# An early one-element Exp, an earlier sum of gelu halves, score banks for a late attention, and a last pair in four banks

## The chip, the cores and the metric

The kernel runs on one core of a Trainium2 chip. The metric is the device time of one execution in microseconds (us). The kernel before was timed three times: 299.24, 299.31 and 299.81 us, median 299.31. Engine names are those of the profile: PE (matmul; PEld is its weight load), DVE (vector), ACT (activation), POOL (GpSimd) and SP, which here only issues DMAs.

## The reference

Attention with a sliding window and 32 global tokens over 8 batches and 8 heads of 64, then a two-layer perceptron with a quick gelu on all 4352 tokens:

```python
s_g   = scale * q_g @ k_all^T            # 32 global rows see all 544 keys
out_g = softmax(s_g) @ v_all
s_l   = [scale * q_l @ k_g^T, where(|i - j| <= 32, scale * q_l @ k_l^T, -1e9)]
out_l = softmax(s_l) @ [v_g, v_l]
x = concat(out_g, out_l) as (B * S, H * D)    # 4352 x 512
h = x @ w_in                                  # 512 -> 2048
g = h / (1 + exp(-1.702 h))
out = g @ w_out                               # 2048 -> 512
```

## The kernel before, in words

The work is cut into phases. A batch i has 512 local tokens. In the first half of its phase (`h_step`, lines 630 to 636) PE makes `hp` for each of 16 slices of d_ff with the weights `w_in_sb` (line 613), and ACT takes each through the gelu into `gT` (line 618). In the second half (`phase_o`, lines 991 to 1046, for i = 2 to 6) PE makes the output of batch i and the attention of batch i+1 and part of i+2, interleaved by hand. The instructions go to each engine in the order in which the Python code writes them (`tc.manual_schedule()`), so a line that stands earlier is earlier in its engine's queue. After batch 7 there is a last stage of the global tokens of all batches (i = B, half as wide), into which the output of batch 7 is interleaved (lines 1082 to 1105), and then one last pair (lines 1107 to 1118).

**The output pairs.** The second matmul layer is done in blocks of two by two with seven products in place of eight. `Pair(i, tt)` has products 1 to 7 (`mm`, line 712), each eight matmuls of 128x256, with sums of gelu halves (`g_sums`, lines 686 and 689, on DVE; index 0, 1, 2 or 3 by line 684) and of weights (`wsum`) as operands. Two PSUM banks hold the four accumulators: `px` has products 3 and 5 in its first half and 4 and 2 in its second, `py` has 1 and 7 in its first half and 6 in its second. Intermediate values are read out between: `m3` (ACT copies product 3 to `zz`, line 113 by way of `on_act`), `z` (line 724, DVE adds the other half of px), `zm` (line 727, adds py), `sub` (line 734), `evict` (ACT copies px to `ob`, line 731, shown as 113), `add` (line 737), `store` (lines 739 to 750: eight DMAs of 32 rows, all issued by SP). Product 5 writes px again, so it waits for `z`; product 7 writes py again and needs g_sums index 3, and waits for `zm`.

**The attention.** `S` (line 558) makes the scores of a group of four heads in the score banks (`spair`), `X` (line 569) takes their Exp on ACT, `M` (line 574) multiplies by the mask, on POOL for round 0 of the later groups (3.3 us) and on DVE for round 1 of the second group (1.0 us). `U(0)` to `U(2)` (line 584) multiply by ones and by the two halves of v, into banks named `ov`, `Gm` (line 595) does the global rows into `og`. `R` (lines 460 to 464) turns the sums of U(0) into reciprocals, `XL` (line 469) scales U(1) and U(2) into `xL`, `G` (lines 474 to 477) does the global rows.

**Banks and tables.** PSUM has eight banks: four in the pool `psP` (`pbank`: hp, px, py, ov, og take turns) and four score banks. A tile that takes a bank waits for the readers of the one before it. ACT loads a table when the function changes between Exp and gelu (1.28 us). `gelu_table` (line 623) calls a gelu on one element to place that load ahead of the next h_step; for Exp the load stands with the first `X` of a phase and takes over its wait.

Of the kernel before, what the change touches and what calls it, by code (L numbers as in the profile page):

```python
# [12 lines left out]
F32 = mybir.dt.float32  # L13
BF16 = mybir.dt.bfloat16
FP8 = mybir.dt.float8e4
AF = mybir.ActivationFunctionType
# [4 lines left out]
def kernel(  # L21
# [12 lines left out]
    nc = tc.nc  # L34

    B, H, Sl, D = q_l.shape
    Sg = q_g.shape[2]
    S = Sg + Sl
    n_tokens = B * S
    d_model = H * D  # L40
# [7 lines left out]
    FC = d_ff // 128  # L48
# [12 lines left out]
    moe = ctx.enter_context(tc.tile_pool(name="moe", bufs=1))  # L61
# [29 lines left out]
    def load_v(b, hs=slice(0, 8)):  # L91
        if b == 2:
            nc.gpsimd.memset(v_view(b, 5)[:, :, :, :, D:], 1.0)
        vt = v_view(b, 5).rearrange("p u j c d -> p (u j) c d")
        vs, vg = (x[b].rearrange("h s d -> s h d") for x in (v_l, v_g))
        for c in range(5):
            n = 128 if c == 2 else 96
            nc.gpsimd.dma_start(out=vt[0:n, hs, c, :D], in_=vs[FIRST[c] : FIRST[c] + n, hs])  # L98
            if c != 2 and b != 1:
                nc.gpsimd.dma_start(out=vt[96:128, :, c, :D], in_=vg)  # L100
# [11 lines left out]
    def on_act(out_, in_):  # L112
        nc.scalar.activation(out_, in_, AF.Copy)  # L113
# [49 lines left out]
    for j in range(4):  # L163
        r = (j + 1) % 4
        nc.gpsimd.memset(bd[32 * r : 32 * r + 32, j, :], 1.0)
    for i in range(2):
# [3 lines left out]
        out=step, in_=step, pattern=[[1, 289]], compare_op=ALU.is_ge,  # L170
# [108 lines left out]
    def pbank(name):  # L279
        return psP.tile([128, 512], F32, name=name, tag="p")  # L280


    def spair():
        return [psS.tile([128, 2, 512], F32, name="s4", tag="s%d" % i) for i in range(2)]

    def bank(pair, j):
        return pair[j // 2][:, j % 2, :]
# [318 lines left out]
    def width(i):  # L606
        return TB if i < B else B * Sg
# [9 lines left out]
    def gelu(out_, in_):  # L617
        nc.scalar.activation(out_, in_, AF.Gelu_apprx_sigmoid)  # L618

    spot = consts.tile([128, 2], F32)  # L620
    nc.gpsimd.memset(spot, 0.0)

    def gelu_table():
        gelu(spot[:, 0:1], spot[:, 1:2])

    def h_act(i, fc, hp):
        n = width(i)
        gelu(gTs[i][:, fc, :n], hp[:, :n])
# [22 lines left out]
    HM = d_model // 2  # L651
# [13 lines left out]
    def parts_of(i):  # L665
        n = width(i)
        t = gTs[i].rearrange("p (g e) t -> p g e t", e=2)
        return [t[:, :, e, h * n // 2 : h * n // 2 + n // 2] for h in range(2) for e in range(2)]

    def g_sums(i, lo, hi, which=(0, 1, 2, 3)):  # L670
        n = width(i)
        if i not in sums:
            if i < B:
                sums[i] = [moe.tile([128, FC // 2, w * HT], BF16, name="gs%d" % k)
                           for k, w in enumerate((1, 1, 2, 1))]
            else:
                room = [ld.tile([128, 2, 16 * D], BF16, name=x).rearrange("p a b -> p (a b)")
                        for x in ("rk", "rq", "rk")]
                sums[i] = [x.rearrange("p (g t) -> p g t", g=FC // 2)
                           for x in (room[0][:, :1024], room[0][:, 1024:], room[1], room[2][:, :1024])]  # L680
        a11, a12, a21, a22 = parts_of(i)
        t = gTs[i].rearrange("p (g e) t -> p g e t", e=2)
        g = slice(lo, hi)
        for k in which:
            if k == 2:
                nc.vector.tensor_tensor(sums[i][2][:, g, :n], t[:, g, 0, :n], t[:, g, 1, :n], ALU.add)  # L686
            else:
                x, y, op = {0: (a11, a22, ALU.add), 1: (a21, a11, ALU.subtract), 3: (a12, a22, ALU.subtract)}[k]
                nc.vector.tensor_tensor(sums[i][k][:, g, : n // 2], x[:, g], y[:, g], op)  # L689

    class Pair:
        def __init__(self, i, tt, banks=None):
            self.i, self.tt = i, tt
            self.banks = banks

        def mm(self, *ks):
            i, tt = self.i, self.tt
            n = width(i) // 2
            a11, a12, a21, a22 = parts_of(i)
            s = sums[i]  # L700
            for k in ks:
                lv, rv, where = {
                    1: (s[0], wsum[0], 2), 2: (s[2][:, :, n : 2 * n], b11, 1), 3: (a11, wsum[1], 0),
                    4: (a22, wsum[2], 1), 5: (s[2], b22, 0), 6: (s[1], wsum[3], 3), 7: (s[3], wsum[4], 2),
                }[k]
                if k == 3:
                    self.x = self.banks[0] if self.banks else pbank("px")
                if k == 1:
                    self.y = self.banks[1] if self.banks else pbank("py")
                out_ = (self.y if where > 1 else self.x)[:, where % 2 * HM : where % 2 * HM + HM]  # L710
                for g in range(FC // 2):
                    nc.tensor.matmul(out_, lhsT=lv[:, g, tt * 128 : tt * 128 + 128], rhs=rv[:, g, :],  # L712
                                     start=(g == 0 and k in (1, 3)), stop=(g == FC // 2 - 1 and k in (2, 5, 6, 7)),
                                     skip_group_check=True)

        def m3(self, eng="act"):
# [19 lines left out]
        def add(self):  # L736
            nc.vector.tensor_add(self.ob[:, 0:4:3], self.zz, self.y.rearrange("p (h m) -> p h m", h=2))

        def store(self):
            for h in range(2):  # L740
                tile_out(self.i, self.tt + h * (width(self.i) // 256), self.ob[:, 2 * h : 2 * h + 2].rearrange("p h m -> p (h m)"))

    def tile_out(i, tci, ob):
        for j in range(4):
            if i < B:
                rows = out[i * S + Sg : (i + 1) * S, :].rearrange("(r t) m -> t r m", t=16)[4 * tci + j]
            else:
                r = (4 * tci + j) * S
                rows = out[r : r + Sg, :]
            nc.sync.dma_start(out=rows, in_=ob[32 * j : 32 * j + 32])  # L750

    obs = {}

# [7 lines left out]
    a, c = Quad(0), Quad(1)  # L761
# [44 lines left out]
    pt = spair()  # L806
# [13 lines left out]
    pt = spair()  # L820
# [27 lines left out]
    a, c = nq[1]  # L848
# [40 lines left out]
    pt = spair()  # L889
# [18 lines left out]
    pt = spair()  # L908
# [3 lines left out]
    a, c = nq[2]  # L912
# [26 lines left out]
    def loads_after(i):  # L939
        if i + 2 < B:  # L940
            load_v(i + 2)
        if i == 1:
            load_g(8, NQ)
        if i + 3 < B:
            load(i + 3)

    def quads_of(n):
        if n < B and n not in nq:
            nq[n] = (Wide(2 * n), Wide(2 * n + 1))
        return nq.get(n, (None, None))  # L950
# [40 lines left out]
    def phase_o(i):  # L991
        b = i + 1
        a, c = nq[b]
        a2, c2 = quads_of(b + 1)
        p0, p1 = Pair(i, 0), Pair(i, 1)
        loads_after(i)
        a.UG()
        c.S(0)
        a.R()
        g_sums(i, 7, 8, (0,))  # L1000
        a.XL(0)
        g_sums(i, 7, 8, (1, 2))
        a.XL(1)
        p0.mm(3, 4, 1)
        c.X(0)
        c.M(0, nc.gpsimd)
        p0.m3()
        p0.z()
        a.G()
        g_sums(i, 7, 8, (3,))  # L1010
        c.S(1)
        c.X(1)
        p0.mm(6)
        p0.zm()
        c.M(1)
        p0.mm(5, 2)
        p0.sub()
        p0.evict()
        p0.mm(7)
        p0.add()  # L1020
        p0.store()
        c.U(0)
        if a2:
            a2.S(0)
            a2.X(0)
            a2.M(0, nc.gpsimd)
        c.U(1)
        c.U(2)
        c.Gm()
        c.RXG()  # L1030
        p1.mm(3, 4)
        p1.m3()
        p1.z()
        p1.mm(1, 6)
        p1.zm()
        if a2:
            a2.S(1)
            a2.X(1)
            a2.M(1, nc.gpsimd)
        p1.mm(5, 2)  # L1040
        p1.sub()
        p1.evict()
        gelu_table()
        p1.mm(7)
        p1.add()
        p1.store()

    for i in range(1, B):
        if i > 1:
            for fc in range(FC):  # L1050
# [3 lines left out]
                if i + 1 < B:  # L1054
                    c = nq[i + 1][1]
# [23 lines left out]
    def pair_banks(k):  # L1079
        return [psX.tile([128, 512], F32, name="x", tag="x%d" % (2 * (k % 2) + j)) for j in range(2)]  # L1080
# [3 lines left out]
    for st in range(FC):  # L1084
        h_step(B, st)
        if st < len(todo):
            tt, k = todo[st]
            if k == 3:
                p = Pair(B - 1, tt, pair_banks(tt))
            p.mm(k)  # L1090
            if k == 4:
                p.m3()
                p.z()
            if k == 6:
                p.zm()
            if k == 2:
                p.sub()
                p.evict()
            if k == 7:
                p.add()  # L1100
                p.store()
        if st in (4, 8, 12):
            g_sums(B, st // 2 - 2, st // 2)
        if st == 14:
            g_sums(B, 6, 7)
    g_sums(B, 7, 8)
    p = Pair(B, 0, pair_banks(0))
    p.mm(3, 4)
    p.m3()
    p.z()  # L1110
    p.mm(1, 6)
    p.zm()
    p.mm(5, 2)
    p.sub()
    p.evict()
    p.mm(7)
    p.add()
    p.store()


# [28 lines left out]
```

## Time and profile before

| what | us |
|---|---|
| median of three runs | 299.31 |
| the profiled execution's own time | 299.64 |
| its span | 297.9 |
| PE busy | 281.3 (94%) |
| DVE busy | 205.1 (69%) |
| ACT busy | 187.9 (63%) |
| POOL busy | 126.7 (43%) |
| ACT table loads | 16, 1.283 each |

The profile is one execution as the hardware profiler saw it. A busy share is that of the whole span. In a timeline each row has the start in us, the duration, the engine, the line, the operation with its tiles and shapes, and in brackets how long the engine had been idle and what ended that. In the chain that ended last, each row is a piece of work, in order of time, that the next one had to wait for. Mean durations of the rows that the change touches: mask on POOL 3.33 (1760 wide), on DVE 1.15 and 1.06; Exp 1.01; product matmul 0.27, starting 0.109 apart; gs of 256 0.25 to 0.28 when nothing holds it; `m3` 0.39, `z` 0.40, `zm` 0.41, `sub` 0.68, `add` 0.69, `evict` 0.60. The phases i = 2 to 6 begin their second half at 102.63, 134.33, about 167.4, about 200.4 and 233.44 us; the last pair's matmuls run from 285.10 to 291.23.

### The profile page before, as it was taken

To read this page: it belongs to the slowest core of one execution; us is meant where nothing else is said; L and a number is where in the kernel's file an instruction comes from. 1 tells how busy PE (TensorE), PEld (TensorE's weight loads), DVE (VectorE), ACT (ScalarE), POOL (GpSimd) and SP (SyncE) were. 2 spreads that over 40 slices of the span, in tenths; PEclk is the share of its full clock that TensorE was granted. 3 is DMA by queue.
4 is the path that set the end of the run, shared out by engine and by line. 5 is a ranking of instruction groups with operands and counts; after the bars stand their busy time and mean duration, and the time that the engine had idled before them with its cause. 6 is when DMAs were issued, how large, how long until landed. Compare 5 with 4: busy or idle time off the path is not lost.

```text
span 297.9 us, 8839 instructions
## 1 busy us (share of the span) xinstructions
PE 281.3 (94%) x3705; PEld 180.3 (61%) x3727; DVE 205.1 (69%) x473; ACT 187.9 (63%) x298; POOL 126.7 (43%) x149
## 2 busy tenths in 40 slices
PE   8899999999999999999999989999999989999990
PEld 7544445444554588547764668447764668458880
DVE  7670268945888997878967986798964886353251
ACT  4857788568677765877468655877377642763320
POOL 8893559786045044952379044923360040000000
PEclk9999999999999999999999999999999999999996
DMA  7999999999959603594129902690121002200222
GB/s 199 163 205 209 204 167 139 188 163 132 197 71 128 116 2 76 87 129 89 29 70 130 150 4 73 97 64 2 47 68 33 2 2 73 70 0 2 70 73 72
DMA packets 59352, 28.24 MB, mean 95 GB/s; under 512 B 47536, under 2 KB 49584, under 8 KB 59312
## 3 DMA queue, kind: packets, MB, share of 16 engines
q0 software_dynamic: 51664, 17.57, 53.5%
q1 hardware_dynamic: 7360, 9.58, 11.7%
q8 instruction: 29, 0.48, 0.7%
q10 hardware_dynamic: 288, 0.52, 0.5%
q14 instruction: 11, 0.09, 0.1%
HBM read 36.31 MB, written 8.91 MB: 152 GB/s over the span
## 4 chain that ended last, share of the span: by engine, by line
PE 69%; DMA 10%; DVE 8%; ACT 4%; POOL 4%; issue 3%; DVEq 0%; POOLq 0%
PE hp L613 33%; PE px L712 7%; PE py L712 7%; PE x L712 6%; PE op L645 6%; PE s L558 4%; PE ov L584 4%; DMA rq<-in_q_l_dram 4%; ACT e L569 3%; DMA w_out_sb<-in_moe_w_out_dram 3%; DVE gs L689 3%; DMA v<-in_v_l_dram 2%; PE s L613 1%; DVE sT L460 1%; DVE xL L469 1%
## 5 line engine op out<-in xcount | busy, mean ns | idle before, releaser
L613 PE MATMUL hp<-xL,w_in_sb 128*128 128x512 bf16 x466 | 104.5, 379 | 1.3 <-DVE xL L469 0.4
L613 PEld LDWEIGHTS <-w_in_sb 128*128 128x128 bf16 x576 | 56.1, 98 | 60.4 <-issue 0.7
L618 ACT ACTIVATE gT<-hp 128x512 bf16<-128x512 f32 x120 | 70.4, 596 | 26.3 <-PE hp L613 24.9
L574 POOL TENSOR_TENSOR e<-e,mask 128x1760 bf16<-128x1760 bf16 (+1 forms) x14 | 46.3, 3304 | 82.7 <-ACT e L569 82.7
L569 ACT ACTIVATE e<-s 128x1016 bf16<-128x1016 f32 (+1 forms) x56 | 53.4, 1006 | 15.2 <-PE s L558 14.8
L689 DVE TENSOR_TENSOR gs<-gT 128x512 bf16<-128x512 bf16 (+1 forms) x90 | 40.2, 472 | 18.8 <-ACT gT L618 18.8
L712 PEld LDWEIGHTS <-gs 128*128 128x128 bf16 x480 | 46.2, 98 | 9.7 <-issue 3.1
L98 POOL DMA_DIRECT2D v<-in_v_l_dram x40 | 31.1, 784 | 16.6 <-PE og L595 12.7
L712 PE MATMUL py<-wsum,gs 128*128 128x256 bf16 x240 | 30.3, 272 | 2.4 <-DVE zz L727 2.4
L645 PE MATMUL op<-w_out_sb,gT 128*128 128x512 bf16 x122 | 28.8, 379 | 0.7 <-issue 0.3
L510 DVE STREAM_TRANSPOSE kT<-rk 128x512 f32<-128x512 f32 x14 | 14.6, 1045 | 9.0 <-DMA rk<-in_k_l_dram 9.0
L645 PEld LDWEIGHTS <-gT 128*128 128x128 bf16 x128 | 11.9, 98 | 14.1 <-issue 0.2
L469 DVE TENSOR_TENSOR xL<-ov,rs 128x512 bf16<-128x512 f32 x29 | 19.1, 685 | 1.0 <-PE ov L436 0.4
L712 PEld LDWEIGHTS <-gT 128*128 128x128 bf16 x192 | 18.0, 98 | 2.8
L712 PE MATMUL px<-w_out_sb,gT 128*128 128x256 bf16 x160 | 19.2, 273 | 0.1
L712 PE MATMUL px<-w_out_sb,gs 128*128 128x256 bf16 x160 | 19.1, 273 | 0.0
L558 PEld LDWEIGHTS <-kT 32*128 32x128 bf16 x672 | 13.3, 93 | 9.6 <-issue 7.4
L113 ACT ACTIVATE ob<-px 128x512 f32<-128x512 f32 x10 | 6.0, 597 | 20.5 <-DVE zz L734 20.5
L574 DVE TENSOR_TENSOR e<-e,mask 128x1712 bf16<-128x1712 bf16 (+1 forms) x14 | 15.7, 1122 | 4.3 <-ACT e L569 4.3
L686 DVE TENSOR_TENSOR gs<-gT 128x1024 bf16<-128x1024 bf16 (+1 forms) x30 | 17.3, 577 | 0.0
L558 PE MATMUL s<-q,kT 32*128 32x160 bf16 (+1 forms) x448 | 15.3, 246 | 0.0
L100 POOL DMA_DIRECT2D v<-in_v_g_dram x24 | 14.1, 589 | 1.6 <-DMA v<-in_v_l_dram 1.6
(140 smaller groups left out, 345.8 us busy)
## 6 DMA issues: line engine op xcount, KB each, us to landing
out_dram<-ob SPq DMA_DIRECT2D x136, 64.0 KB, 1.7
rq<-in_q_l_dram POOLq DMA_DIRECT2D x5, 512.0 KB, 7.3
rk<-in_k_l_dram POOLq DMA_DIRECT2D x5, 512.0 KB, 9.0
v<-in_v_l_dram POOLq DMA_DIRECT2D x24, 96.0 KB, 4.1
w_in_sb<-in_moe_w_in_dram POOLq DMA_DIRECT2D x8, 256.0 KB, 7.9
w_out_sb<-in_moe_w_out_dram POOLq DMA_DIRECT2D x4, 512.0 KB, 10.2
rq<-in_q_l_dram POOLq DMA_DIRECT2D x5, 256.0 KB, 6.2
rk<-in_k_l_dram POOLq DMA_DIRECT2D x5, 256.0 KB, 6.2
```

The costliest lines, as they stand in the source:

```text
L98: nc.gpsimd.dma_start(out=vt[0:n, hs, c, :D], in_=vs[FIRST[c] : FIRST[c] + n, hs])
L469: nc.vector.tensor_mul(self.x[:, 2 * self.u + h, :], self.st[1 + h], self.st["rs"])
L510: nc.vector.transpose(flat[:, 0:Sl].rearrange("p (r t) -> p t r", t=16), loaded[self.b][0][:, self.u].bitcast(F32))
L558: nc.tensor.matmul(bank(self.ps, j)[:, at : at + n], lhsT=self.k[p, KEYS[c] : KEYS[c] + 128, e], rhs=qs[p, :, :, e], start=(e == 0), stop= ...
L569: nc.scalar.activation(self.E[rnd][:, 2 * i : 2 * i + 2, :n], self.ps[i][:, :, :n], AF.Exp, scale=scale)
L574: eng.tensor_mul(e, e, mask[:, rnd : rnd + 1, :n].to_broadcast([128, 4, n]))
L613: nc.tensor.matmul(hp[:, : width(i)], lhsT=w_in_c[:, fc // 4, kc, fc % 4 // 2, :, fc % 2], rhs=(xL[i] if i < B else xG)[:, kc, :], start=( ...
L618: nc.scalar.activation(out_, in_, AF.Gelu_apprx_sigmoid)
L645: nc.tensor.matmul(op, lhsT=gTs[i][:, fc, tci * 128 : tci * 128 + 128], rhs=w_out_sb[:, fc, :], start=(first and fc == 4 * f4), stop=(fc = ...
L686: nc.vector.tensor_tensor(sums[i][2][:, g, :n], t[:, g, 0, :n], t[:, g, 1, :n], ALU.add)
L689: nc.vector.tensor_tensor(sums[i][k][:, g, : n // 2], x[:, g], y[:, g], op)
L712: nc.tensor.matmul(out_, lhsT=lv[:, g, tt * 128 : tt * 128 + 128], rhs=rv[:, g, :], start=(g == 0 and k in (1, 3)), stop=(g == FC // 2 - 1 ...
```

## The change

1. A new `exp_table()` calls an Exp on one element. `phase_o` calls it first, behind the last gelu of the batch.
2. In `phase_o` the sum of index 3 for the last slices (`g_sums(i, 7, 8, (3,))`) moves from behind `a.G()` to directly behind `a.XL(1)`, ahead of `p0.m3()` and `p0.z()`.
3. In the last `phase_o` (i = 6, where there is no further batch), U(0), U(1), U(2) and Gm of the second group go to four score banks instead of `pbank`s.
4. `store` can name the engine that issues each half. The second pair of batch 7 gives its second half to ACT's queue; it is written in step 13 of the last stage, ahead of the gelus of steps 14 and 15.
5. The last pair has four banks, one for each accumulator, the order of products 3, 4, 1, 6, 2, 5, 7 (before: 3, 4, 1, 6, 5, 2, 7), and stores its output in three pieces: the second tile by SP (four DMAs of 64 KB), then the second column half of the first tile by POOL and its first column half by ACT (four of 32 KB each).

```diff
+    def exp_table():
+        nc.scalar.activation(spot[:, 0:1], spot[:, 1:2], AF.Exp)
...
+            self.apart = banks and len(banks) == 4
...
+                if self.apart:
+                    out_ = self.banks[where][:, :HM]
...
-                                     start=(g == 0 and k in (1, 3)), stop=(g == FC // 2 - 1 and k in (2, 5, 6, 7)),
+                                     start=(g == 0 and k in ((1, 3, 4, 6) if self.apart else (1, 3))), stop=(g == FC // 2 - 1 and k in (2, 5, 6, 7)),
...
-        def store(self):
+        def store(self, engs=(nc.sync, nc.sync)):
...
+        def quarter(self, h, m, eng):
+            tile_out(self.i, self.tt + h, self.ob[:, 2 * h + m], eng, slice(m * HM, m * HM + HM))
...
         loads_after(i)
+        exp_table()
         a.UG()
         c.S(0)
         a.R()
...
         a.XL(1)
+        g_sums(i, 7, 8, (3,))
         p0.mm(3, 4, 1)
         c.X(0)
         c.M(0, nc.gpsimd)
         p0.m3()
         p0.z()
         a.G()
-        g_sums(i, 7, 8, (3,))
...
-        c.U(0)
         if a2:
+            c.U(0)
...
+        else:
+            pt = spair()
+            c.U(0, bank(pt, 0))
+            c.U(1, bank(pt, 2))
+            c.U(2, bank(pt, 3))
+            c.Gm(bank(pt, 1))
...
-                p.store()
+                p.store((nc.sync, (nc.sync, nc.scalar)[tt]))
...
-    p = Pair(B, 0, pair_banks(0))
-    p.mm(3, 4)
-    p.m3()
-    p.z()
-    p.mm(1, 6)
-    p.zm()
-    p.mm(5, 2)
-    p.sub()
-    p.evict()
+    x0, y0 = pair_banks(0)
+    y1, x1 = pair_banks(1)
+    p = Pair(B, 0, (x0, x1, y0, y1))
+    zz = [moe.tile([128, HM], F32, name="zz%d" % k) for k in range(2)]
+    p.ob = moe.tile([128, 4, HM], F32, name="ob", bufs=3)
+    p.mm(3)
+    on_act(zz[0], x0[:, :HM])
+    p.mm(4)
+    nc.vector.tensor_add(zz[0], zz[0], x1[:, :HM])
+    p.mm(1)
+    nc.vector.tensor_add(zz[1], zz[0], y0[:, :HM])
+    p.mm(6)
+    nc.vector.tensor_add(zz[1], zz[1], y1[:, :HM])
+    p.mm(2)
+    nc.vector.tensor_sub(p.ob[:, 3], zz[1], x1[:, :HM])
+    on_act(p.ob[:, 2], x1[:, :HM])
+    tile_out(B, 1, p.ob[:, 2:4].rearrange("p h m -> p (h m)"))
+    p.mm(5)
+    nc.vector.tensor_sub(zz[0], zz[0], x0[:, :HM])
+    on_act(p.ob[:, 1], x0[:, :HM])
+    p.quarter(0, 1, nc.gpsimd)
     p.mm(7)
-    p.add()
-    p.store()
+    nc.vector.tensor_add(p.ob[:, 0], zz[0], y0[:, :HM])
+    p.quarter(0, 0, nc.scalar)
```

More of the change, by code (lines that the diff above doesn't have):

```diff
@@ L705, in mm @@
                 }[k]
[L706 to L710, printed above, removed]
+                if self.apart:
+                    out_ = self.banks[where][:, :HM]
+                else:
+                    if k == 3:
+                        self.x = self.banks[0] if self.banks else pbank("px")
+                    if k == 1:
+                        self.y = self.banks[1] if self.banks else pbank("py")
+                    out_ = (self.y if where > 1 else self.x)[:, where % 2 * HM : where % 2 * HM + HM]
                 for g in range(FC // 2):
                     nc.tensor.matmul(out_, lhsT=lv[:, g, tt * 128 : tt * 128 + 128], rhs=rv[:, g, :],
-                                     start=(g == 0 and k in (1, 3)), stop=(g == FC // 2 - 1 and k in (2, 5, 6, 7)),
+                                     start=(g == 0 and k in ((1, 3, 4, 6) if self.apart else (1, 3))), stop=(g == FC // 2 - 1 and k in (2, 5, 6, 7)),
                                      skip_group_check=True)
@@ L737, in add, with tile_out @@
             nc.vector.tensor_add(self.ob[:, 0:4:3], self.zz, self.y.rearrange("p (h m) -> p h m", h=2))
-        def store(self):
+        def store(self, engs=(nc.sync, nc.sync)):
             for h in range(2):
-                tile_out(self.i, self.tt + h * (width(self.i) // 256), self.ob[:, 2 * h : 2 * h + 2].rearrange("p h m -> p (h m)"))
-    def tile_out(i, tci, ob):
+                tile_out(self.i, self.tt + h * (width(self.i) // 256),
+                         self.ob[:, 2 * h : 2 * h + 2].rearrange("p h m -> p (h m)"), engs[h])
+        def quarter(self, h, m, eng):
+            tile_out(self.i, self.tt + h, self.ob[:, 2 * h + m], eng, slice(m * HM, m * HM + HM))
+    def tile_out(i, tci, ob, eng=nc.sync, cols=slice(0, d_model)):
         for j in range(4):
             if i < B:
-                rows = out[i * S + Sg : (i + 1) * S, :].rearrange("(r t) m -> t r m", t=16)[4 * tci + j]
+                rows = out[i * S + Sg : (i + 1) * S, cols].rearrange("(r t) m -> t r m", t=16)[4 * tci + j]
             else:
                 r = (4 * tci + j) * S
-                rows = out[r : r + Sg, :]
-            nc.sync.dma_start(out=rows, in_=ob[32 * j : 32 * j + 32])
+                rows = out[r : r + Sg, cols]
+            eng.dma_start(out=rows, in_=ob[32 * j : 32 * j + 32])
     obs = {}
@@ L1026, in phase_o @@
             a2.M(0, nc.gpsimd)
-        c.U(1)
-        c.U(2)
-        c.Gm()
+            c.U(1)
+            c.U(2)
+            c.Gm()
+        else:
+            pt = spair()
[3 more added lines that the diff above has]
+            c.Gm(bank(pt, 1))
         c.RXG()
```

## The prediction

> **What bounds the kernel now.** I read the page's busy shares first, then the chain that ended last in order of time, then the timelines of DVE, POOL, ACT and SP around the edits.
>
> ```profile
> PE 281.3 (94%) x3705; PEld 180.3 (61%) x3727; DVE 205.1 (69%) x473; ACT 187.9 (63%) x298; POOL 126.7 (43%) x149
> ```
>
> PE is busy 94% of the 297.9 us span, so only what makes PE wait or run longer counts, and what stands behind PE's last matmul. The waits by pair put three kinds of PE wait inside the phases that the diff touches: py behind DVE zz L727 (2.4 us, 4 times), s behind ACT e L569 (1.9 us, 4 times), and 0.32 us behind ACT ob L113, once. The chain shows one of the four phases (i=3):
>
> ```profile
> 135.76 0.63 PE s L558 x23
> 136.53 1.18 issue
> 137.71 1.93 ACT e L569 x2
> 139.63 0.29 ACT zz L113
> 139.94 0.42 DVE zz L724
> ...
> 141.04 2.22 DVE gs L689
> 143.25 0.34 DVE zz L727
> 143.64 1.03 PE py L712 x8
> ```
>
> Two things are to be seen. "issue" is the load of the Exp table, which waits with the first Exp for the scores. And gs L689, 0.25 us elsewhere, takes 2.2. ACT, DVE and POOL say why:
>
> ```profile
> 134.44 0.60 ACT L618 ACTIVATE gT<-hp 128x512 bf16<-128x512 f32 x1 [0.27 <-PE hp L613]
> 136.41 1.28 ACT L569 ACT_TABLE_LOAD   x1 [1.38 <-PE s L558]
> 137.71 1.93 ACT L569 ACTIVATE e<-s 128x1016 bf16<-128x1016 f32 x2
> ...
> 138.19 0.68 DVE L469 TENSOR_TENSOR xL<-ov,rs 128x512 bf16<-128x512 f32 x1
> 140.96 2.29 DVE L689 TENSOR_TENSOR gs<-gT 128x256 bf16<-128x256 bf16 x1
> ...
> 139.79 3.32 POOL L574 TENSOR_TENSOR e<-e,mask 128x1760 bf16<-128x1760 bf16 x1 [8.97 <-ACT e L569]
> ```
>
> POOL masks from 139.79 to 143.11; the DVE sum, with two inputs from SBUF, ends 0.14 us behind it. DVE operations with one input from PSUM (zz L724) run beside POOL at their usual 0.42 us. So a gs that meets a running mask waits until the mask ends.
>
> I count from the start of ov in a phase (134.33 here). Phase i=2 has its table load early by chance (103.35) and lasts 17.79 us (102.63 to 120.42) without a PE wait; phase 3 lasts 19.13. Phases 4 to 6 repeat phase 3's waits. So **1.34 us a phase** is what the table load costs, four times.
>
> **Part 1: the table load.** Last gelu at +0.11, its successor 0.62 later (103.35 behind 102.73), the load 1.28, the one-element Exp 0.11 to its successor (122.38 to 122.49 for the gelu twin). So X(0) starts at +2.13 instead of +3.38; the scores are there at +2.08. In phase 2 it moves from +2.04 to +2.13. POOL's mask starts 2.08 us behind X(0) (139.79 - 137.71): at **+4.21** in every phase.
>
> **Part 2: the sum of halves moved ahead.** g_sums(3) now stands on DVE directly behind xL of half 1 and ahead of zz L724. In phases 2 to 5 DVE works without a gap up to there, and the instruction behind xL starts 0.60 after it (106.49 to 107.09): 138.19 + 0.60 is **+4.46**, 0.25 us behind the new start of the mask. By the rows above it then waits for the mask: the mask ends at 4.21 + 3.32 = 7.53, gs at 7.67, zz L724 starts at 7.60 (0.07 overlap, as L727 today), and PE can go on 0.46 later (143.18 to 143.64), at 8.06. Who waits for zz L724? In the order of the changed program the first px matmul of product 5 does, as before; it was ready at +6.11 in phase 2 (108.74) and +6.79 in phase 3. Products 5 and 2 take 1.86 (108.74 to 110.60), so product 7 starts at 9.92. Today it starts at 7.97 in phase 2 and 9.31 in phase 3. Behind gs stand also G (1.02 from z's start) and zz L727, ready at 9.08, which is in time; M(1) at 8.95 to 9.98 is in time for U(0) at 10.88. So phase 2 **loses 1.95**, phases 3, 4 and 5 **lose 0.61 each** (1.83): the 1.34 is gained and 1.95 lost.
>
> Phase 6 is different: DVE is not behind there.
>
> ```profile
> 233.55 0.60 ACT L618 ACTIVATE gT<-hp 128x512 bf16<-128x512 f32 x1 [0.27 <-PE hp L613]
> 237.04 0.68 DVE L469 TENSOR_TENSOR xL<-ov,rs 128x512 bf16<-128x512 f32 x1
> ```
>
> gs(3) can start at 237.04 + 0.60 = 237.64, the mask at 233.55 + 0.62 + 1.28 + 0.11 + 0.02 + 2.08 = 237.66: a tie. If DVE has it, the phase runs like phase 2 today, 1.34 shorter; if POOL, 0.61 longer. I give the tie to DVE, which is 0.02 earlier by the rows.
>
> The trace shows no gs that starts within 0.3 us of a mask. The bounds for one phase are therefore 0.28 us (gs finds the port free) and 3.2 us (it meets the whole mask); I take the second in phases 2 to 5, as the rows that waited (2.12 and 2.29) waited to the mask's end whenever POOL had started first. The Trainium skill, SBUF — State Buffer, "Who interferes with whom", says that whoever issues first holds the shared pair for its whole instruction; by it the 0.25 us decide everything, as in my sum. The Trainium skill, Perfetto Trace Analysis, "Per-engine timelines", puts POOL's shown start at its first read, but DVE's shown start behind its fetch; that speaks for POOL in phases 2 to 5, with a margin somewhat under 0.25, and for DVE in phase 6. No row here shows either.
>
> **Part 3: last attention in score banks (phase 6).** U(2) waits 0.32 for the eviction of px, and px of the second pair starts at 245.72, 0.06 behind sT L460. Three U and Gm take 1.36 from ov to s (134.33 to 135.69); from 243.72 that is 245.08, 0.64 earlier. But product 5 of that pair waits for zz L724, 249.07 today, and starts at 249.29. DVE's row up to there doesn't move against U(0): **0.17 gained** where DVE had the tie; the whole 0.64 where POOL had it, since U(0) is then late against DVE.
>
> **Part 4: stores and the last pair.** The second store of the pair before the last goes half to ACT's queue. It stands ahead of the gelus of steps 14 and 15 and waits for ob L737 (284.50 + 0.68 = 285.18).
>
> ```profile
> 0.81 0.95 ACTq L149 DMA_DIRECT2D early<-in_k_l_dram  x2
> 1.79 1.28 ACT L768 ACT_TABLE_LOAD   x1 [1.79 <-PEq L1133]
> ...
> 284.22 1.30 ACT L618 ACTIVATE early<-hp 128x256 bf16<-128x256 f32 x3
> 285.24 10.37 SPq L750 DMA_DIRECT2D out_dram<-ob  x16
> ```
>
> Two DMAs on ACT took 0.95, and its next instruction started behind them at 1.79: ACT stands still while it issues. Four from 285.24 at 0.46 (eight on SP take 3.61) end at 287.08, so the gelu of step 14, done today by about 285.1, ends at 287.47. PE needs it for the last group of product 3: resumed at 287.6 with 0.11 of that product and six at 0.87 to go, it ends at 292.95, not 291.23. **1.72 lost.** This wait is new, and nothing covers it.
>
> Then the gain: instead of one 0.69 add and eight stores behind the end (292.00, last one at 295.20, landing 1.7 later, 1.0 more to the span's end), a 0.42 add and four on ACT: first 293.44, last 294.82, landed 296.5, span 297.5. Quarter (0,1) goes over POOL: product 5 ends at 292.07, sub 0.42, ob 0.39, with hand-overs POOL starts at 293.1; four at 0.57 (v_g issues of 0.59), the last at 294.8. A store from POOL isn't in the trace: bounds 1.7 (SP's stores) and 3.1 (the fastest quiet v load from POOL) give 297.5 to 298.9. I take 1.9, near the stores, because SP loads of 64 KB take 3.3 to 4.2, like POOL's loads: the direction, not the queue, makes the difference. Span 297.7: **0.2 gained** in all, between 0.4 gained and 1.0 lost. The Trainium skill, DMA: Bandwidth & Descriptors, "Latency and other measured facts", has the first byte from POOL 0.4 us later than from SP; by it, as an estimate, the span would end at 297.9.
>
> **Sum** on the profiled execution (299.64 us, span 297.9): +1.95 + 1.83 - 1.34 - 0.17 - 0.2 = +2.1, so 301.7. The median shown is 299.31, 0.33 lower; with the same difference, **301.4**.
>
> **Rivals.**
> - *POOL has phase 6 too.* +0.61 - 0.64 in place of -1.34 - 0.17: 1.48 more, **302.9**. For it: a 0.02 us margin; against it: DVE is first by the rows.
> - *DVE has the port in every phase* (the faster side). It decides if the mask reads its first element over 0.25 us behind its shown start. Two forms of the mask (1760 and 1712 wide, 3328 and 3246 ns) differ by 1.7 ns an element, which leaves some 0.3 us of each mask for start and end together, so this isn't far off. Then phase 2 is level, phases 3 to 6 gain 1.34 each, with 0.17 and 0.2: -5.7, **293.6**. Against it: 0.25 is nearly all of that 0.3, and part of it lies at the end, where a gs ends 0.14 behind the mask.
> - *ACT goes on while it issues.* Then PE ends at 291.23 and everything behind comes 1.7 earlier: 301.4 - 1.7 = **299.7**. Only the 1.79 row speaks against it.
> - *The change doesn't do what it says*: the Exp may not move the load. Then the mask stays at +5.46 in phases 3 to 6, gs at +4.46 is free and zz L727 comes 2.1 earlier: they keep the wait of 0.47 and lose the one of 0.66. Phase 2, whose load is early anyway, loses 1.86 (mask at +4.12): 1.86 - 4 x 0.66 - 0.4 = -1.2, **298.1**. Against it: the order of the changed program has the load directly behind the last gelu, without a wait.
>
> **Chances.** Forecast 0.46, POOL in phase 6 too 0.22, ACT goes on 0.08, DVE everywhere 0.18, the last 0.01, else 0.05. The range takes the first three with POOL's landing at its far bound: 299.5 to 304.0. A difference under 0.2% (0.6 us) can't be told from none; faster 0.20, within 0.07, slower 0.73.
>
> **What would show it.** In phases 2 to 5 gs L689 behind the second xL lasts about 3.2 us, and PE px waits about 1.95 behind zz L724; the mask starts 4.2 behind ov. In phase 6 that gs lasts 0.28. ACT's early rows of the last two gelus start near 287.1 plus the shift, 1.8 us behind the store's issue; PE's first x matmuls of the last pair show a wait of about 1.7 behind ACT. It is wrong if gs lasts 0.28 in phases 2 to 5 (time near 293.6), or if ACT's gelus run beside its DMA issues.

## The result, and the profile after

| | us |
|---|---|
| before, median of 4 runs beside the changed kernel | 299.27 (299.11 to 299.81) |
| after, median of 4 runs | 302.59 (301.57 to 302.93) |
| ratio | 1.0102, 95% interval 1.0075 to 1.0129 |
| profiled execution after: own time, span | 302.54, 300.8 |

The changed kernel takes 1.0% longer by the ratio, 3.3 us between the medians; 301.4 us was forecast, 2.1 more than before. First the busy shares of the page of after:

```profile
PE 281.8 (94%) x3727; PEld 179.5 (60%) x3727; DVE 207.5 (69%) x475; ACT 188.5 (63%) x304; POOL 128.8 (43%) x153
```

PE's busy time is nearly what it was (281.3 before) and the span grew by 2.9, so PE mostly waits longer. The waits by pair of after say for whom (total, times, longest, in us):

```profile
PE px L719 <- DVE zz L731: 7.6, 5, 1.8
...
PE x L719 <- ACT early L618: 1.7, 1, 1.7
```

Before, the phases had 2.4 behind zm and 1.9 behind the Exp. Both are gone, and 7.6 behind `z` (now line 731) and 1.7 behind a gelu have come. The timeline of phase 3 (the same phase as in the prediction; ov starts at 136.40) shows the first of them:

```profile
137.12 1.28 ACT L627 ACT_TABLE_LOAD   x1
138.41 0.20 ACT L627 ACTIVATE spot<-spot 128x1 f32<-128x1 f32 x1
138.52 1.91 ACT L569 ACTIVATE e<-s 128x1016 bf16<-128x1016 f32 x2
...
140.58 3.31 POOL L574 TENSOR_TENSOR e<-e,mask 128x1760 bf16<-128x1760 bf16 x1 [7.74 <-ACT e L569]
140.87 3.18 DVE L692 TENSOR_TENSOR gs<-gT 128x256 bf16<-128x256 bf16 x1
...
143.97 0.41 DVE L731 TENSOR_TENSOR zz<-zz,px 128x256 f32<-128x256 f32 x1
...
144.43 1.91 PE L719 MATMUL px<-w_out_sb,gs 128*128 128x256 bf16 x16 [1.75 <-DVE zz L731]
```

The load stands directly behind the last gelu, the Exp no longer waits for it, and the mask starts at +4.18. The moved sum starts 0.29 behind the mask and ends 0.16 behind the mask's end (140.58 + 3.31 = 143.89); `z` is queued behind it on DVE, and product 5 waits 1.75 for `z`. The chain that ended last runs through the same rows (start, us, what):

```profile
140.35 0.60 DVE xL L469
140.95 3.10 DVE gs L692
144.05 0.34 DVE zz L731
...
144.43 1.91 PE px L719 x16
```

In phase 6 the two operations start within 0.03 us of each other, and the sum is not held (timeline of after):

```profile
241.07 3.48 POOL L574 TENSOR_TENSOR e<-e,mask 128x1760 bf16<-128x1760 bf16 x1 [15.29 <-ACT e L569]
241.10 0.28 DVE L692 TENSOR_TENSOR gs<-gT 128x256 bf16<-128x256 bf16 x1
...
251.33 1.91 PE L719 MATMUL px<-w_out_sb,gs 128*128 128x256 bf16 x16 [0.57 <-DVE zz L731]
```

Here the mask is the longer one, by 0.16. The kernels of experiments 5, 6 and 8 have the same tie in their phase 6: there too the sum starts 0.02 to 0.03 behind the mask, isn't held, and the mask lasts 3.48 to 3.49. The last row is new as well: product 5 of the second pair waits 0.57 for its `z`. The tail, in the timeline of after (a queue's row, ACTq, gives the time in which the DMAs were issued):

```profile
286.54 0.68 DVE L744 TENSOR_TENSOR ob<-zz,x 128x512 f32<-128x512 f32 x1
...
287.29 1.79 ACTq L761 DMA_DIRECT2D out_dram<-ob  x4
...
289.13 0.66 ACT L618 ACTIVATE early<-hp 128x256 bf16<-128x256 f32 x2 [2.50 <-issue]
289.57 1.16 PE L719 MATMUL x<-w_out_sb,early 128*128 128x256 bf16 x9 [1.67 <-ACT early L618]
...
295.39 2.07 POOL L761 DMA_DIRECT2D out_dram<-ob  x4 [50.83 <-ACT ob L113]
...
295.58 1.78 ACTq L761 DMA_DIRECT2D out_dram<-ob  x4
```

ACT starts no gelu between 286.26 and 289.13, and PE stands for 1.67. Of ACT's 2.50 without work about 0.65 is the store's wait for its data (`ob`, done at 287.22) and 1.79 the issue of its four DMAs. PE ends at 295.10 and the span 5.73 later (6.7 before). What ends last are the instructions by which the program closes, by operation (shortest, median and longest in ns, then the first and last start):

```profile
L1174 POOLq DRAIN  x3: 46/102/3347, 296.7 to 300.6; - x3
L1174 SPq DRAIN  x3: 7/7/7, 299.0 to 300.3; - x3
```

Each engine's queue closes with such DRAINs. SP's first one starts at 299.0, when every store has landed. POOL's stands behind its last store; by the rows it starts at 296.7, while that store is still being issued (POOL's row ends at 297.46), lasts 3.35 us and ends at 300.05, 1.0 behind SP's.

**Where the 2.9 us of span come from**, against before: the start +0.26 (ov of phase 2 at 102.89 instead of 102.63; with the same code up to there it comes anywhere from 101.85 to 103.37 in the profiled executions of all the kernels here, so this isn't put down to the change), phases 2 to 5 +3.20 (ov of phase 2 to ov of phase 6: 134.01 after, 130.81 before), phase 6 to the next `hp` -1.42 (17.05 and 18.47), PE's wait behind the gelu +1.85 (8.13 from the last pair's first matmul to PE's end, 6.28 before, counted from 284.94; the 285.10 given for it ahead of the prediction is 0.16 late), from there to the end -1.0. The sum is +2.9.

### The profile page after: what moved, and what is told of

Its sections match the earlier page's. It is cut to its first block, busy times and chain, and to the rows that moved or that the text cites. A ratio compares the mean times of both kernels' runs of the same rounds, so it can differ in the third digit from the quotient of the medians.

```text
span 300.8 us, 8861 instructions
## 1 busy us (share of the span) xinstructions
PE 281.8 (94%) x3727; PEld 179.5 (60%) x3727; DVE 207.5 (69%) x475; ACT 188.5 (63%) x304; POOL 128.8 (43%) x153
## 4 chain that ended last, share of the span: by engine, by line
PE 69%; DVE 23%; ACT 3%; DMA 1%; issue 1%; ACTq 1%; POOL 1%; POOLq 0%; DVEq 0%
PE hp L613 27%; PE px L719 9%; PE op L648 8%; DVE gs L692 8%; PE py L719 6%; PE x L719 5%; PE s L558 4%; DVE xL L469 3%; PE ov L584 3%; DVE gs L689 2%; PE s L613 2%; DVE rs L464 2%; DVE sT L460 2%; DMA g32q<-in_q_g_dram 1%; DVE kT L510 1%
## 5 line engine op out<-in xcount | busy, mean ns | idle before, releaser
L692 DVE TENSOR_TENSOR gs<-gT 128x512 bf16<-128x512 bf16 (+1 forms) x90 | 41.8, 491 | 18.6 <-ACT gT L618 18.5
L648 PE MATMUL op<-w_out_sb,gT 128*128 128x512 bf16 x128 | 29.5, 380 | 0.0
L761 POOL DMA_DIRECT2D out_dram<-ob x4 | 2.1, 534 | 50.8 <-ACT ob L113 50.8
L469 DVE TENSOR_TENSOR xL<-ov,rs 128x512 bf16<-128x512 f32 x27 | 17.9, 686 | 0.9 <-PE ov L436 0.4
```

The costliest lines, as they stand in the source:

```text
L469: nc.vector.tensor_mul(self.x[:, 2 * self.u + h, :], self.st[1 + h], self.st["rs"])
L648: nc.tensor.matmul(op, lhsT=gTs[i][:, fc, tci * 128 : tci * 128 + 128], rhs=w_out_sb[:, fc, :], start=(first and fc == 4 * f4), stop=(fc = ...
```

## The experiments

The theory was that the loss is made by the order of two starts on the port that DVE and POOL share, and by ACT's DMA issues; rivals were that something else in the change makes PE wait, and those of the prediction. Each kernel was timed beside the kernel before, all but one of them several times. The ratios are to that kernel; its median moves between 299.11 and 299.46 from one experiment to another, so a difference of two medians is good to some tenths of a us.

**1. Part 2 undone.**

```diff
         a.XL(1)
-        g_sums(i, 7, 8, (3,))
...
         a.G()
+        g_sums(i, 7, 8, (3,))
```

> The changed kernel with part 2 alone undone: g_sums(3) stands behind G again. Theory (the sum meets the running mask and holds up zz ahead of product 5): zz comes 3 us earlier in phases 2 to 5, product 5 waits for nothing, each of these phases runs as phase 2 did before (17.8 us), 1.8 less in each of four: 302.6 - 7.2 = 295.4. gs still lasts some 2.1 us, but behind zz. Rival (what hurts is the mask that starts earlier, wherever the sum stands): the wait of product 5 stays and the time is within 0.6 of 302.6.

294.89 us (294.55 to 296.3), ratio 0.9851 (0.9825 to 0.9877). One line that is moved back is worth 7.7 us between the medians, 7.5 by the ratios. The timeline of phase 3 of this kernel:

```profile
137.81 3.31 POOL L574 TENSOR_TENSOR e<-e,mask 128x1760 bf16<-128x1760 bf16 x1 [7.74 <-ACT e L569]
138.09 0.41 DVE L731 TENSOR_TENSOR zz<-zz,px 128x256 f32<-128x256 f32 x1
...
139.10 2.17 DVE L692 TENSOR_TENSOR gs<-gT 128x256 bf16<-128x256 bf16 x1
```

The sum still meets the mask and is still held until it ends, but `z` stands ahead of it, and all phases take 31.77 us. So it isn't the hold that costs, but what is queued behind the held instruction.

**2. The sum earlier still**, with the other sums ahead of `XL(1)`:

```diff
-        g_sums(i, 7, 8, (1, 2))
+        g_sums(i, 7, 8, (1, 2, 3))
         a.XL(1)
-        g_sums(i, 7, 8, (3,))
```

> The changed kernel with g_sums(3) one step further ahead, in front of xL of half 1: it starts some 0.3 us ahead of the mask instead of 0.28 behind it. Theory: gs lasts 0.28 us, the mask waits for nothing that shows, product 5 waits for nothing in phases 2 to 5: about 295.2. Rival (sums of halves are slow at this place for another reason, such as the Exp that runs on ACT): gs is still slow, and the time stays near 302.6.

294.28 (293.9 to 295.65), ratio 0.9831 (0.9805 to 0.9857), phases of 31.58. In its timeline of phase 3 the sum starts 0.32 ahead of the mask and is free:

```profile
138.30 0.28 DVE L692 TENSOR_TENSOR gs<-gT 128x256 bf16<-128x256 bf16 x1
138.50 0.68 DVE L469 TENSOR_TENSOR xL<-ov,rs 128x512 bf16<-128x512 f32 x1
138.62 3.32 POOL L574 TENSOR_TENSOR e<-e,mask 128x1760 bf16<-128x1760 bf16 x1 [7.74 <-ACT e L569]
```

**3 and 4. The start of the mask shifted.** `exp_table()` is called two times, or three times, in place of once. This moves only POOL's mask; the sum's place stays that of the change.

```diff
         exp_table()
+        exp_table()
```

> The changed kernel with two one-element Exps in place of one: X(0) and the mask start 0.11 us later, 0.18 ahead of gs instead of 0.28. If the port goes to the instruction whose shown start is first: no change, 302.6, gs 3.1 us. If a mask takes the port only 0.2 us behind its shown start: gs lasts 0.28 in phases 2 to 5, and the time is near 295.4. In phase 6 of the changed kernel gs started 0.03 behind the mask's shown start and was not held, so the point lies between 0.03 and 0.28.

> The changed kernel with three one-element Exps: the mask starts 0.07 us ahead of gs. If the port goes to the instruction whose shown start is first, phases 2 to 5 still wait: 302.6. If the point lies anywhere from 0.07 to 0.28, gs lasts 0.28 there and the time is near 295.4, although ACT has 0.22 us more to do in each phase.

Two: 305.38 (304.38 to 306.04), ratio 1.0201 (1.0167 to 1.0234). Three: 294.55 (294.12 to 295.93), ratio 0.984 (0.9808 to 0.9871). An extra Exp delays the mask by about 0.23 us, not by the 0.11 counted, so two didn't quite reach the other order. The timeline of phase 4 with two:

```profile
174.16 3.32 POOL L574 TENSOR_TENSOR e<-e,mask 128x1760 bf16<-128x1760 bf16 x1 [7.88 <-ACT e L569]
174.22 3.41 DVE L692 TENSOR_TENSOR gs<-gT 128x256 bf16<-128x256 bf16 x1
...
178.01 3.46 PE L719 MATMUL px<-w_out_sb,gs 128*128 128x256 bf16 x16 [1.99 <-DVE zz L731]
```

and of phase 3 with three:

```profile
139.05 0.28 DVE L692 TENSOR_TENSOR gs<-gT 128x256 bf16<-128x256 bf16 x1
139.24 3.32 POOL L574 TENSOR_TENSOR e<-e,mask 128x1760 bf16<-128x1760 bf16 x1 [8.24 <-ACT e L569]
```

Starts 0.04 to 0.06 behind the mask were held for the whole mask in phases 2 to 5 of the kernel with two; 0.03 behind (phase 6 of after) and 0.19 ahead were not. A quarter of a microsecond of work that nobody uses takes 10.8 us off the time. That settles the mechanism: with the sum at the same place, which of the two starts first decides whether it is held.

The kernel with two met neither of its expectations, 302.6 and 295.4: it takes longer than both. PE's stall is 1.99 instead of 1.75, and in phase 4 more is lost than that. Busy time of PE in that kernel by stretch (stretch, PE busy with matmul count, granted clock, DMA share, GB/s):

```profile
177.00:178.00 1.00, 0.00 (x0) 0.91 0.00 0
178.00:179.00 1.00, 0.99 (x5) 0.50 0.00 0
179.00:180.00 1.00, 1.00 (x7) 0.50 0.00 0
180.00:181.00 1.00, 1.00 (x7) 0.50 0.00 0
181.00:182.00 1.00, 1.00 (x10) 0.88 0.00 0
```

From about 177.8 the clock is at 0.50 for 3.4 us, and the sixteen px matmuls take 3.46 instead of 1.91. The equal wait in phase 2 of the same execution has no such stretch behind it:

```profile
110.55 1.91 PE L719 MATMUL px<-w_out_sb,gs 128*128 128x256 bf16 x16 [1.99 <-DVE zz L731]
```

Phase 4 lasts 35.3 us, phases 2, 3 and 5 last 33.7. The profiled execution took 304.38, the shortest of the four; what makes the others longer isn't shown.

**5. The stores of the pair before the last all on SP.**

```diff
-                p.store((nc.sync, (nc.sync, nc.scalar)[tt]))
+                p.store()
```

> The changed kernel with all eight stores of the pair before the last on SP again. Theory (ACT stands still while it issues four DMAs, and the gelus of steps 14 and 15 come late): PE's wait of 1.67 behind ACT early is gone, 302.6 - 1.7 = 300.9. Rival (the last product would wait for SP's second half of stores, or the last gelu is late for another reason): within 0.5 of 302.6.

299.68 (299.37 to 300.36), ratio 1.0015 (1.0002 to 1.0027). In its timeline the three gelus run on, and the product behind them has no wait:

```profile
285.74 1.30 ACT L618 ACTIVATE early<-hp 128x256 bf16<-128x256 f32 x3
```

From the last pair's first matmul to PE's end it takes 6.28 again. So the expected 1.7 came, and the rival is out. Of the 2.9 us between the medians (2.6 by the ratios) the trace explains 1.85 by this; the profiled executions also differ by 0.6 at the start. What makes the rest between the medians stays open.

**6. POOL's quarter on SP.**

```diff
-    p.quarter(0, 1, nc.gpsimd)
+    p.quarter(0, 1, nc.sync)
```

> The changed kernel with the quarter that POOL stores given to SP. The profile of the changed kernel ends 1.7 us behind the last store's landing, and POOL's drain ends at 300.05 although all stores have landed by 299.1. Theory (the drain behind POOL's own DMA issues holds the end): SP's last issue starts near 297.4, lands at 299.1, the span ends at 300.1, 0.7 earlier: 301.9. Rival (the end is 1.7 behind the last landing in any case): no change or later, 302.6 to 303.

301.21 (300.84 to 303.92), ratio 1.0079 (1.0052 to 1.0105). The closing instructions of this kernel:

```profile
L1174 POOLq DRAIN  x3: 51/102/5561, 240.5 to 299.5; - x3
L1174 SPq DRAIN  x3: 7/7/7, 298.9 to 299.2; - x3
```

POOL's first DRAIN now starts at 240.5, beside other work, and the end comes 5.2 behind PE's end instead of 5.73. These 0.5 us are what the trace gives to this edit, where 0.7 was expected; the rest of the 1.4 between the medians isn't explained.

**7. The Exp alone**: before, with part 1 and nothing else.

```diff
         loads_after(i)
+        exp_table()
```

> The kernel before with the early one-element Exp alone. Theory: phases 3 to 6 run like phase 2 does already, 1.34 less each: 299.3 - 5.4 = 293.9. Rival (an earlier mask costs what the earlier load gains): within 0.6 of 299.3.

294.4 (293.89 to 294.45), ratio 0.9832 (0.9809 to 0.9856), phases of 31.77 to 31.80. Part 1 brings 4.7 us by itself (299.11 to 294.4 in this experiment), where 5.4 was expected. The rival that an earlier mask costs what the load gains is out, and so is the prediction's rival that the load doesn't move.

**8. No score banks**: U and Gm of the last attention in their banks of before, the rest as changed; one run.

```diff
+        c.U(0)
         if a2:
-            c.U(0)
...
-            pt = spair()
-            c.U(0, bank(pt, 0))
...
+        c.U(1)
+        c.U(2)
+        c.Gm()
```

> The changed kernel with U and Gm of the last phase in the four shared banks again. Theory: U(2) waits for the eviction of px as before, but product 5 waits for zz with or without that; phase 6 (236.90 to 253.95 in the changed kernel, 17.05 us) is some 0.2 longer, and the time 302.8. Rival (the whole wait of 0.64 was gained): 17.7 us and 303.2.

301.56 us, one run, which by itself tells nothing apart. But phase 6 takes 16.82 here and 17.05 after, and the wait of 0.57 behind `z` is not there. Theory and rival both had this phase longer without score banks, so both missed. DVE's transpose of the row sums in phase 6 of before, then of after, and then in this kernel:

```profile
244.95 0.71 DVE L460 STREAM_TRANSPOSE sT<-ov 128x512 f32<-128x512 f32 x1
```

```profile
247.22 0.72 DVE L460 STREAM_TRANSPOSE sT<-s 128x512 f32<-128x512 f32 x1 [0.38 <-PE s L595]
```

```profile
246.10 0.71 DVE L460 STREAM_TRANSPOSE sT<-ov 128x512 f32<-128x512 f32 x1
```

It starts 1.23 behind the first U before, 1.49 in after, and 1.03 here. The four score banks are parts of one tile (`pt`), and the transpose is released by Gm (line 595), which writes that tile last; in banks of its own it is free once U(0) is done.

**9, 10 and 11. All together.** `combo` has edits 2, 5 and 6; `combo_old_tail` also has the last pair of before, in two banks; `combo_no_banks` is `combo` with edit 8.

> The changed kernel with three edits: the sum of the last gelu halves in front of XL(1), all eight stores of the pair before the last on SP, the quarter (0, 1) on SP. If the three faults found are separate (gs held behind POOL's mask; ACT standing still while it issues four DMAs, 1.85 us; POOL's queue emptied late, about 0.6 us net), they add up: 294.3 (the kernel with the earlier sum alone) - 1.85 - 0.6 = 291.8 us. Rival: they share the slack at the end (SP's own queue with twelve late issues becomes the last), so that the two edits at the end bring only the first one's 1.85 or less: 292.5 to 293.0. Phases of 31.58 us and no wait of PE behind zz or behind early by both.

> The kernel combo with the last pair as before (two banks, evictions and stores in two halves). If the last pair in four banks is worth what its end shows (5.2 us from PE's end to the end in place of 6.7), 291.8 + 1.5 = 293.3 us. Rival: the end is set by the landing of the last store and the queues' emptying alike in both, then 291.8 to 292.2.

> The kernel combo with the last attention in its own banks as before (no score banks). By the trace of the changed kernel, where DVE's transpose of the last quad's sums (L460) starts only behind the group's matmuls (L595) that now write into the same tile, score banks make zz of the second pair late and PE waits about 0.2 to 0.6 us there: without them the kernel is 0.2 to 0.6 us faster than combo, 291.2 to 291.6 by the sum of combo. Rival, as predicted: score banks spare 0.17 us of waits for banks, and without them it takes 0.17 more, 292.0.

| kernel | us | ratio | interval |
|---|---|---|---|
| combo | 292.33 (291.79 to 292.97) | 0.9758 | 0.9729 to 0.9788 |
| combo_old_tail | 293.68 (293.06 to 295.72) | 0.9816 | 0.9781 to 0.985 |
| combo_no_banks | 291.87 (291.39 to 294.08) | 0.9755 | 0.9721 to 0.9789 |

`combo` lies between its two expectations. The wait behind the gelu is gone, so the 1.85 came whole; of the 0.6 the end shows 0.2 (5.5 us behind PE's end, 5.7 in experiment 2). The wait of 0.57 behind `z` in phase 6, which the expectation had ruled out, is still there. The timeline of the end:

```profile
284.79 3.88 SPq L761 DMA_DIRECT2D out_dram<-ob  x8
...
286.07 1.86 ACTq L761 DMA_DIRECT2D out_dram<-ob  x4
```

SP issues the eight stores of its part until 288.67 and ACT its four until 287.93, so SP is the last. It is done 3.1 behind PE's end here and 2.8 in experiment 6, where the end comes 5.2 behind; why its issues take longer here isn't shown. The last pair in four banks is worth 1.35 between the medians, but the intervals of the two ratios overlap; from PE's end to the end it is 5.5 against 6.7, 1.2. Without score banks phase 6 takes 16.64 instead of 17.05, the transpose starts 0.86 behind U(0) instead of 1.50, and the wait behind `z` is gone; the medians differ by 0.46, with intervals that overlap. `combo_no_banks` has the lowest median, 2.4% under before; `combo` isn't told apart from it by time.

## Why the prediction was right, point by point

- **Part 1, the mask at +4.21**: measured +4.18 in phase 3 (140.58 - 136.40) and +4.19 in phase 2. Right. What the load costs was put at 1.34 a phase; in experiment 7 it is 1.27 (33.04 to 31.77).
- **Part 2, the sum held in phases 2 to 5**: right in each of the four: the starts are 0.28, 0.29, 0.42 and 0.29 apart where 0.25 was forecast. Forecast was a loss of 1.95 in phase 2 and 0.61 in each of the next three, 3.78 in all; measured 1.81 (33.51 against 31.70) and 0.47, 0.46 and 0.47: **3.20**. The mis-sized term is "Products 5 and 2 take 1.86 (108.74 to 110.60)". That row of before held a wait of 0.1 for `zm` at its end; without one the sixteen matmuls take 1.75 (144.43 to 146.18), so product 7 starts 0.11 earlier in every phase. Another 0.03 is that PE goes on at +8.03 and not at +8.06.
- **Phase 6, the tie to DVE**: right, but with luck. The reason given was that DVE is 0.02 earlier by the rows; by the shown starts it was 0.03 behind, and it still wasn't held. No row of before could decide this. Phase 6 to the next `hp` came 1.42 shorter where 1.34 + 0.17 were forecast. The Trainium skill, SBUF — State Buffer, "Who interferes with whom", says that the first to issue holds the shared pair for its whole instruction. The traces agree, with this limit: the shown starts tell who was first only to about 0.05 us (0.03 behind was free, 0.04 behind was held).
- **Part 3, 0.17 gained**: wrong in sign. The step that failed is "DVE's row up to there doesn't move against U(0)": it does, since the transpose starts 1.49 behind U(0) and no longer 1.23, and product 5 waits for `z`, which comes at the end of that row. The prediction counted who waits for a bank and not who waits for the tile. With the sum free, score banks lose 0.23 (after) to 0.41 (`combo`) in phase 6; where the sum is still behind `z` they make no difference (17.21 in experiment 1, 17.19 in experiment 7).
- **Part 4, ACT stands still while it issues**: right, 1.72 forecast, 1.85 measured; experiment 5 takes it away by moving the four DMAs. ACT needs 0.45 for each and starts the next gelu only behind the fourth. So the rival that ACT goes on while it issues is out. The row of before on which the step rested (the table load at 1.79) was weak for it, since it names PEq as what released the load.
- **Part 4, the end**: 4.75 from PE's end to the end of the span was forecast (292.95 to 297.7), 5.73 came. POOL's stores landed 2.0 behind their issue (1.9 taken). Missing was POOL's DRAIN. In after it ends 2.6 behind POOL's last issue; before it stood behind the last mask, beside other work:

```profile
L1144 POOLq DRAIN  x3: 51/102/5409, 238.9 to 297.7; - x3
```

 In these rows of DMA issues in after (KB each, then median us from issue to landing):

```profile
out_dram<-ob ACTq DMA_DIRECT2D x4, 64.0 KB, 2.1
out_dram<-ob POOLq DMA_DIRECT2D x4, 32.0 KB, 2.0
out_dram<-ob ACTq DMA_DIRECT2D x4, 32.0 KB, 1.7
```

 POOL's stores are 0.3 slower than ACT's of the same size. The 0.4 that the Trainium skill, DMA: Bandwidth & Descriptors, "Latency and other measured facts", gives for the first byte is near that.
- **The sum**: +2.1 was forecast on the profiled execution and +2.9 came, made of -0.6 in phases 2 to 5, +0.1 in phase 6 with the score banks, +0.1 at ACT, +1.0 at the end and +0.26 at the start. The errors upwards are 1.5 and the one downwards is 0.6, so it is in part luck that the total is only 0.8 off. Between the medians it is 1.2 off.

By kernels, as ratios to before: part 1 alone has 0.9832; with parts 3 and 4 it is 0.9851, which isn't told apart from that; with part 2 as well it is 1.0102, some 7.5 us more. Part 1 alone is a gain, and by the rows of before part 2 alone would put the sum about 1 us ahead of the mask in phases 3 to 6; no run has it alone. It was part 1 that moved the mask to where part 2 puts the sum.

## What to carry to other kernels

When an instruction is moved up on an engine, look at what is queued behind it and at everything that may hold it at its new place, a port included; here 0.3 us decided over 7.7. Where two engines share a port, place the short operation well ahead of the long one, or behind all that is urgent. A store issued by ACT cost ACT the wait for its data and the issue time, and a late one by POOL put POOL's DRAIN at the end, so late in this kernel neither was a free queue.

## What the hardware showed that was not expected

- A PE wait of about 2 us can cost more than itself. In the profiled executions a stretch at half clock, 3.4 us long, followed one of the three waits of 1.98 and 1.99 us with two Exps, and the waits of 2.03, 2.25 and 2.29 us (for q, at the start of `combo_old_tail`, after and three Exps). It followed none of the waits up to 1.76. The Trainium skill, TensorE: Matmul & The Clock Gate, "Part 1: The HAM clock gate (the "warmup" mystery)", puts the fall behind an idle window of about 3.4 us. Here the runs decide: 2 us can be enough, and need not be. What decides between two equal waits isn't shown.
- One-element Exps in a row cost 0.23 each behind the first, not the 0.11 that one takes up to its successor. Here they all write the same element; whether that is the reason isn't shown.
- POOL's closing DRAIN ended 2.5 to 2.6 us behind the end of POOL's last store issue in the seven kernels where it stands behind one (297.45 and 300.05 in after), and 2.0 to 2.1 behind the end of its last mask in before and in experiments 6 and 7. What it does in that time isn't shown. The program doesn't end before it.
